# A parallel linear-attention and MLP kernel: later input tiles loaded behind the DMA transposes, the statistics of each tile finished before the previous tile is normalised, and the first MLP units of some tiles split

## The chip, the cores and the metric

The kernel runs on one core of one Trainium2 chip. The metric is the device time of one execution in microseconds (us); lower is better. The span of a profile, from its first to its last instruction, is about 1.75 us shorter than the time of the same execution. All runs compared here are in the fast state (granted TensorE clock 1.0) except one profile, which is named where it comes up.

## The reference, cut to what matters

```python
xn = layernorm(x)                      # x: 2048 x 640, bf16, eps 1e-5
out = x + attention(xn) + mlp(xn)      # both read the same normalised x
# attention: qkv = xn @ wqkv; phi(q), phi(k) with phi(t) = elu(t) + 1 + 1e-6;
#            32 heads of 20; o = phi(q) (phi(k)^T v) / (phi(q) sum phi(k) + 1e-6); o @ wo
# mlp:       gelu(xn @ w1 + b1) @ w2 + b2,  w1: 640 x 1536
```

## The kernel before

The 2048 rows are 16 tiles of 128. A tile goes through this line of stations before TensorE can use it: a load of x (SyncE's DMA queue), two `bn_stats` halves and a `bn_aggr` (VectorE), epsilon and the power -1/2 (GpSimd), the normalisation (VectorE), and a transposition into `xnT` (by TensorE for tiles 0 to 2, by DMA on SyncE's queue for tiles 3 to 15). While the tiles arrive, TensorE computes the first MLP product in units: one block of 128 of the 1536 features for one, two or four tiles. Each engine works through its own list in order (in the profile of before, VectorE normalises tile 7 only at 24.39 us, behind its wait for tile 8, although the rstd of tile 7 was there at 19.18), so the order in which the program writes its calls is the schedule.

```python
def ln_half(t, h):                 # VectorE: statistics of one half of tile t
    bn_stats(stats[:, s, ...], x_in[:, t, half h])
    if t < 2 and h == 0:           # GpSimd: epsilon goes in ahead of the aggregate (tiles 0, 1)
        stats[:, s, 2:3] += D * EPS
def ln_aggr(t):
    bn_aggr(aggr[:, s, :], stats[:, s, :])             # VectorE
    if t < 2: var = aggr[:, s, 1:2]
    else:     var = aggr[:, s, 1:2] + EPS              # GpSimd, all other tiles
    rstd[:, t] = var ** -0.5                           # GpSimd

# ... MLP units of tiles 0-3, one tile each ...
for t, n in ((4, 2), (6, 2), (8, 4), (12, 4)):         # then pairs, then fours
    plan += h_list(t, n, 0, JT)                        # JT = 12 feature blocks

def ln_rest():                     # called after tile 3
    for t in range(4, NT):
        if t + 1 < NT:
            ln_half(t + 1, 0); ln_half(t + 1, 1)
        ln_norm(t)
        if t + 1 < NT:
            ln_aggr(t + 1)
        xnT_dma(t)                 # DMA transpose
        if t == 5:
            dma_x(8, 4); dma_x(12, 4)
# ... (cut) then K, G, Q, the output product ...
```

Note that with this order the statistics of tile 8 stand ahead of the normalisation of tile 7 in VectorE's list.

## Time and profile before

| | before |
|---|---|
| median of the first 3 runs | 207.9 us (207.6 to 208.03) |
| the profiled execution | 208.43 us, span 206.7 us |
| TensorE busy | 98% of the span |
| MLP phase (first MLP matmul to the first K matmul) | 6.74 to 60.79 us |

The busy line of the page (busy time, share of the span, instructions):

```profile
PE 202.7 (98%) x1614; PEld 138.0 (67%) x1614; DVE 109.6 (53%) x227; ACT 73.6 (36%) x148; POOL 34.5 (17%) x85
```

TensorE bounds the kernel, so only its holes can be won. Matmul rows hide short holes: the profile's own legend says that the ends of matmuls are modelled, and the row at 34.73 below runs to 60.79 us, 0.17 us into the next, which starts at 60.62. So in the two views below, the matmul row at 34.73 admits 0.48 us of idling before it where the weight loads show 0.74, and the hole of 0.26 us at 27.24 is in no matmul row at all. The timeline of the matmuls, then that of the weight loads (start us, duration us, engine, line, operation, tiles; in brackets the idle time before the row and what ended it):

```profile
11.48 22.76 PE L388 MATMUL ps<-xnT,W 128*128 128x128 bf16 x285
34.73 26.06 PE L388 MATMUL ps<-xnT,W 128*128 128x512 bf16 x120 [0.48 <-DMA xnT<-xn_tm]
60.62 1.66 PE L490 MATMUL ps<-Wqkv,xnT 128*128 128x320 bf16 x11
```

```profile
11.43 15.81 PEld L388 LDWEIGHTS ps<-xnT,W 128*128 128x128 bf16 x225
27.50 6.46 PEld L388 LDWEIGHTS ps<-xnT,W 128*128 128x128 bf16 x60 [0.26 <-issue]
34.70 25.59 PEld L388 LDWEIGHTS ps<-xnT,W 128*128 128x128 bf16 x120 [0.74 <-issue]
```

The first 225 loads are the units of tiles 0-3 and of the pair 4-5, the next 60 the pair 6-7, the last 120 tiles 8-15. So TensorE waits at the pair 6-7 and again at tiles 8-11. VectorE's timeline shows why tile 7 is late (here and below, ... stands for rows left out):

```profile
17.66 0.45 DVE L361 TENSOR_SCALAR xn_tm<-xPK,aggr,rstd 128x640 bf16<-128x640 bf16 x1 [0.32 <-POOL rstd L349]
18.02 0.20 DVE L341 BATCH_NORM_AGGREGATE aggr<-stats 128x2 f32<-128x12 f32 x1
23.59 0.89 DVE L333 BATCH_NORM_STATS2 stats<-xPK 128x6 f32<-128x320 bf16 x2 [5.37 <-DMA xPK<-in_A_x_dram]
24.39 0.43 DVE L361 TENSOR_SCALAR xn_tm<-xPK,aggr,rstd 128x640 bf16<-128x640 bf16 x1
...
26.01 0.45 DVE L361 TENSOR_SCALAR xn_tm<-xPK,aggr,rstd 128x640 bf16<-128x640 bf16 x1 [0.32 <-POOL rstd L349]
```

The rows of L361 are the normalisations of tiles 6, 7 and 8. Tile 7 (24.39) had its statistics at 18.2, but waits for x8, for which VectorE idles 5.37 us. The 0.32 us before the other normalisations is the wait for rstd; it is part of the spacing of 1.63 us from tile to tile.

To measure holes I use one number for each profile, the *stretch*: from the end of TensorE's transposition of tile 2 to the start of K. Two lines of the chain of waits give its start and another its end (start us, duration us, what):

```profile
11.37 0.29 PE ps L369 x5
...
60.79 21.73 PE ps L490 x160
```

Here it is 60.79 - 11.66 = 49.13 us.

### The profile page before, as it was taken

The page shows a single profiled execution, that of the slowest core. Times are in us where ns is not written, and L with a number is a line of the kernel's source. Part 1 is how long each engine was busy: PE and PEld are TensorE (multiplying, and loading weights), DVE is VectorE, ACT ScalarE, POOL GpSimd, SP SyncE. Part 2 cuts the span into 40 slices and gives each one's busy share as a digit, 9 for nine tenths or more (in the row PEclk, how much of TensorE's full clock was granted, in tenths as well). Part 3 has the DMA queues.
Part 4 walks back from the last instruction along what each step waited for, and adds up shares of the span by engine and source line. Part 5 has one row for each costly group of instructions (what it writes and reads, how often), then busy time and mean ns, then how long its engine had stood idle before and what let it go on. Part 6 is the DMA issues. An engine that isn't in the chain of part 4 may idle for free.

```text
span 206.7 us, 4035 instructions
## 1 busy us (share of the span) xinstructions
PE 202.7 (98%) x1614; PEld 138.0 (67%) x1614; DVE 109.6 (53%) x227; ACT 73.6 (36%) x148; POOL 34.5 (17%) x85
## 2 busy tenths in 40 slices
PE   8999999999999999999999999999999999999995
PEld 3899886444457777777746445677777777777774
DVE  3784477100006888999448888744863322523322
ACT  2799886666667544211143554300000000000000
POOL 3233144710000000999100200000000000000000
DMA  5968975599920000000000000978611110010012
GB/s 149 347 175 75 278 100 101 97 353 324 376 86 0 0 3 0 3 0 0 0 3 2 0 0 10 342 202 165 164 67 52 43 35 32 32 36 32 32 36 62
DMA packets 24827, 19.70 MB, mean 95 GB/s; under 512 B 9960, under 2 KB 24808, under 8 KB 24808
## 3 DMA queue, kind: packets, MB, share of 16 engines
q1 hardware_dynamic: 23056, 17.86, 30.1%
q10 hardware_dynamic: 1752, 1.58, 4.1%
q8 instruction: 13, 0.21, 0.4%
q14 instruction: 6, 0.05, 0.1%
HBM read 13.11 MB, written 2.62 MB: 76 GB/s over the span
## 4 chain that ended last, share of the span: by engine, by line
PE 85%; DMA 5%; DVE 3%; POOL 3%; issue 2%; SPq 0%; ACT 0%; DVEq 0%
PE ps L673 36%; PE ps L388 15%; PE ps L490 11%; PE ps L515 11%; PE ps L556 10%; DMA xPK<-in_A_x_dram 4%; POOL rstd L349 2%; DVE stats L333 1%; DMA xnT<-xn_tm 1%; DVE aggr L341 1%; PE ps L610 1%; DVE xn_tm L361 1%; PE ps L566 1%; POOL veps L347 1%; PE ps L620 1%
## 5 line engine op out<-in xcount | busy, mean ns | idle before, releaser
L673 PE MATMUL ps<-W,HG 128*128 128x320 bf16 (+2 forms) x396 | 54.8, 295 | 0.0
L388 PE MATMUL ps<-xnT,W 128*128 128x128 bf16 (+2 forms) x480 | 53.3, 272 | 0.6 <-DMA xnT<-xn_tm 0.5
L388 PEld LDWEIGHTS ps<-xnT,W 128*128 128x128 bf16 x480 | 36.7, 98 | 16.6 <-issue 1.2
L673 PEld LDWEIGHTS ps<-W,HG 128*128 128x128 bf16 x396 | 38.1, 98 | 14.5 <-ACT Msb L592 0.2
L392 ACT ACTIVATE HG<-ps,b1c 128x128 bf16<-128x128 f32 (+2 forms) x96 | 41.5, 475 | 13.1 <-PE ps L388 11.5
L684 DVE TENSOR_TENSOR W<-ps,xnT 128x640 bf16<-128x640 f32 x15 | 12.4, 825 | 35.6 <-PE ps L673 35.0
L478 ACT ACTIVATE ek<-ps 128x512 bf16<-128x512 f32 (+1 forms) x36 | 23.2, 645 | 20.4 <-PE ps L556 10.3
L479 DVE TENSOR_SCALAR ek<-ek 128x512 bf16<-128x512 bf16 (+1 forms) x36 | 10.9, 304 | 31.9 <-ACT ek L478 30.7
L673 PE MATMUL ps<-Msb,PQ 128*128 128x320 bf16 (+2 forms) x165 | 24.2, 295 | 0.0
L556 PE MATMUL ps<-xnT,Wqkv 128*128 128x512 bf16 x100 | 21.9, 379 | 0.0
L490 PE MATMUL ps<-Wqkv,xnT 128*128 128x320 bf16 x160 | 21.9, 299 | 0.0
L515 PE MATMUL ps<-xPK,xn_tm 128*128 128x320 bf16 x160 | 21.9, 299 | 0.0
L673 PEld LDWEIGHTS ps<-Msb,PQ 128*128 128x128 bf16 x165 | 15.9, 98 | 5.9
L490 PEld LDWEIGHTS ps<-Wqkv,xnT 128*128 128x128 bf16 x160 | 15.7, 98 | 6.2
L515 PEld LDWEIGHTS ps<-xPK,xn_tm 128*128 128x128 bf16 x160 | 15.7, 98 | 6.1
L509 POOL COPY Wqkv<-Wqkv 128x128 bf16<-128x128 bf16 x25 | 15.1, 603 | 22.9 <-PE ps L490 21.4
L333 DVE BATCH_NORM_STATS2 stats<-xPK 128x6 f32<-128x320 bf16 x32 | 13.7, 467 | 8.7 <-DMA xPK<-in_A_x_dram 8.6
L556 PEld LDWEIGHTS ps<-xnT,Wqkv 128*128 128x128 bf16 x100 | 9.7, 98 | 11.4
L481 DVE SCALAR_TENSOR_TENSOR PQ<-ps,ek 128x512 bf16<-128x512 f32 x20 | 13.8, 691 | 2.1
L481 DVE SCALAR_TENSOR_TENSOR xPK<-ps,ek 128x640 bf16<-128x640 f32 x16 | 13.2, 825 | 1.7
L527 DVE TENSOR_TENSOR Msb<-Msb,xPK 128x640 f32<-128x640 f32 x14 | 11.6, 825 | 0.5
L519 ACT ACTIVATE W<-ps 128x640 bf16<-128x640 f32 x5 | 3.5, 704 | 18.2 <-PE ps L515 18.2
(59 smaller groups left out, 83.5 us busy)
## 6 DMA issues: line engine op xcount, KB each, us to landing
xnT<-in_A_x_dram SPq DMA_DIRECT2D x4, 640.0 KB, 6.3
Wqkv<-in_A_wqkv_dram SPq DMA_DIRECT2D x3, 800.0 KB, 6.9
out_dram<-W SPq DMA_DIRECT2D x15, 160.0 KB, 1.8
W<-in_B_w_dram SPq DMA_DIRECT2D x4, 480.0 KB, 6.0
W<-in_B_w_dram SPq DMA_DIRECT2D x1, 1920.0 KB, 13.3
xn_tm<-rden ACTq DMA_DIRECT2D x12, 128.0 KB, 3.4
xPK<-in_A_x_dram SPq DMA_DIRECT2D x2, 640.0 KB, 5.8
Wo<-in_A_wo_dram SPq DMA_DIRECT2D x8, 160.0 KB, 8.8
```

The lines of the kernel that those rows point to most:

```text
L333: Pl.ins(v, lambda e: e.bn_stats(stats[:, s, 6 * h:6 * h + 6], x_in[:, t, h * HW:(h + 1) * HW]), reads=r_x[t], writes=[r_stats[s][h]])
L388: Pl.ins(pe, [(lambda e, k=k: e.matmul(bank(b, 0, w), W1[:, k, jb * P:(jb + 1) * P], xnT[:, k, tok], start=(k == 0), stop=(k == DT - 1))) ...
L392: Pl.ins(s_, lambda e: e.activation(HG[:, jb, tok], bank(b, 0, w), ACT.Gelu_apprx_tanh, bias=b1c[:, jb:jb + 1]), reads=[B_[b], r_b1c], wri ...
L478: Pl.ins(s_, lambda e: e.activation(e2, src, ACT.Exp), reads=br, writes=[r_ek[s]])
L481: Pl.ins(v, lambda e: e.scalar_tensor_tensor(out=d2, in0=src, scalar=0.0, in1=e2, op0=ALU.max, op1=ALU.add), reads=br + [r_ek[s]], writes= ...
L490: fns.append(lambda e, k=k, h=h, b=b, t=t: e.matmul(bank(b + h, 0, HW), xnT[:, k, t * P:(t + 1) * P], Wqkv[:, k, D + h * HW:D + (h + 1) * ...
L509: Pl.ins(g, lambda e, k=k, i=i: e.tensor_copy(plain(Wqkv[:, k, D:2 * D], i), parts(Wqkv[:, k, 0:D], i)), reads=[r_Wq], writes=[r_Wk, r_WqP])
L515: Pl.ins(pe, [(lambda e, t=t, h=h, b=b, f=f, i=i: e.matmul(bank(b + h, 0, HW), xn_tm[:, t, f * P:(f + 1) * P], PK[:, t, h * HW:(h + 1) * H ...
L527: Pl.ins(v, lambda e, t=t: e.tensor_tensor(out=zsum, in0=zsum, in1=PK[:, t, :], op=ALU.add), reads=[r_PK[t], r_zsum], writes=[r_zsum])
L556: Pl.ins(pe, [(lambda e, k=k, j=j, b=b: e.matmul(bank(b), Wqkv[:, k, D + j * P:D + (j + 1) * P], xnT[:, k, cc], start=(k == 0), stop=(k == ...
L673: Pl.ins(pe, [(lambda e, i=i, x=x, bb=bb: e.matmul(bank(bb, 0, x[1] - x[0]), seq[i][0], seq[i][1][:, x[0]:x[1]], start=(i == 0), stop=(i = ...
L684: Pl.ins(v, lambda e: e.tensor_tensor(out=halves(out_sb[:, s, :]), in0=pair(b), in1=halves(x_res[:, t, :]), op=ALU.add), reads=B_[b:b + 2] ...
```

## The change

Its intent is to let the transposes of tiles 3-7 go ahead of the x8-15 loads, to give each rstd a whole tile of time (the statistics of tile t+1 are finished before tile t is normalised: one tile ahead), and to start tiles 4-5 and 8-11 on fewer tiles, so that the first units need fewer of them. The epsilon goes in ahead of the aggregate for every tile. The diff, cut to its core:

```diff
-            if t < 2 and h == 0:
+            if h == 0:
                 Pl.ins(g, lambda e: e.tensor_single_scalar(stats[:, s, 2:3], ..., D * EPS, ALU.add), ...)
...
-        for t, n in ((4, 2), (6, 2), (8, 4), (12, 4)):
-            plan += h_list(t, n, 0, JT)
+        plan += h_list(4, 1, 0, 2) + h_list(5, 1, 0, 2) + h_list(4, 2, 2, JT) + h_list(6, 2, 0, JT)
+        plan += h_list(8, 2, 0, 3) + h_list(10, 2, 0, 3) + h_list(8, 4, 3, JT) + h_list(12, 4, 0, JT)
 
         def ln_rest():
-            for t in range(4, NT):
-                ... (as shown above)
+            def out(t):
+                ln_norm(t)
+                xnT_dma(t)
+            ln_stats(5)
+            out(4)
+            ln_stats(6)
+            out(5)
+            ln_stats(7)
+            out(6)
+            out(7)
+            dma_x(8, 2)
+            dma_x(10, 2)
+            dma_x(12, 4)
+            ln_stats(8)
+            for t in range(8, NT):
+                if t + 1 < NT:
+                    ln_stats(t + 1)
+                out(t)
```

More of the change, by code (lines that the diff above doesn't have):

```diff
@@ L175, in bass_parallel_sum__linear_attn_block__dense_activation_gelu__prompt_kernel @@
         aggr = sb("aggr", [P, 4, 2], FP32)
-        veps = sb("veps", [P, 4], FP32)
         rstd = sb("rstd", [P, NT], FP32)
@@ L221, in bass_parallel_sum__linear_attn_block__dense_activation_gelu__prompt_kernel @@
         r_aggr = [R_("aggr%d" % i) for i in range(4)]
-        r_veps = [R_("veps%d" % i) for i in range(4)]
         r_rstd = [R_("rstd%d" % i) for i in range(NT)]
@@ L342, in ln_aggr @@
                    reads=r_stats[s], writes=[r_aggr[s]])
-            if t < 2:
-                var, r_var = aggr[:, s, 1:2], r_aggr[s]
-            else:
-                var, r_var = veps[:, s:s + 1], r_veps[s]
-                Pl.ins(g, lambda e: e.tensor_single_scalar(var, aggr[:, s, 1:2], EPS, ALU.add),
-                       reads=[r_aggr[s]], writes=[r_var])
-            Pl.ins(g, lambda e: e.tensor_tensor(out=rstd[:, t:t + 1], in0=var, in1=mhalf[:], op=ALU.pow),
-                   reads=[r_var, r_small], writes=[r_rstd[t]])
+            Pl.ins(g, lambda e: e.tensor_tensor(out=rstd[:, t:t + 1], in0=aggr[:, s, 1:2], in1=mhalf[:], op=ALU.pow),
+                   reads=[r_aggr[s], r_small], writes=[r_rstd[t]])
         def ln_stats(t):
@@ L419, in bass_parallel_sum__linear_attn_block__dense_activation_gelu__prompt_kernel @@
         plan += h_list(0, 1, 9, JT) + h_list(1, 1, 9, JT) + h_list(3, 1, 0, JT)
-        for t, n in ((4, 2), (6, 2), (8, 4), (12, 4)):
-            plan += h_list(t, n, 0, JT)
+        plan += h_list(4, 1, 0, 2) + h_list(5, 1, 0, 2) + h_list(4, 2, 2, JT) + h_list(6, 2, 0, JT)
+        plan += h_list(8, 2, 0, 3) + h_list(10, 2, 0, 3) + h_list(8, 4, 3, JT) + h_list(12, 4, 0, JT)
         def ln_rest():
-            for t in range(4, NT):
-                if t + 1 < NT:
-                    ln_half(t + 1, 0)
-                    ln_half(t + 1, 1)
-                ln_norm(t)
-                if t + 1 < NT:
-                    ln_aggr(t + 1)
-                xnT_dma(t)
-                if t == 5:
-                    dma_x(8, 4)
-                    dma_x(12, 4)
+            def out(t):
[13 more added lines that the diff above has]
+            for t in range(8, NT):
+                if t + 1 < NT:
+                    ln_stats(t + 1)
+                out(t)
         for u in plan:
```

## The prediction

> **What bounds the kernel now.** TensorE. The busy table gives PE 202.7 of 206.7 us (98%), and the chain of waits puts 85% on it. From 6.74 us its matmuls are almost unbroken there. The change touches only the MLP phase (line 388, 6.74 to 60.79 us), so only holes in those 54.05 us can be won.
>
> **The holes.** Back to back the matmuls cost 56 ns at width 128 (60 in 3.35 us in the chain) and 217 ns at width 512 (120 in 26.06 us). [...] The 128-wide units end at about 20.7 us (165 x 56 ns after 11.48). The 120 matmuls of width 256 should then take 13.1 us, but the first of width 512 starts at 34.73, so about 0.85 us are lost. The weight loads in the timeline show where: a hole of 0.26 us at 27.24 to 27.50 (tiles 6-7), one of 0.74 us ending at 34.70 (tiles 8-11; the matmul row admits only 0.48 of it, because ends are modelled).
>
> The first hole is tile 7. Its normalisation stands in the vector engine's order behind the statistics of tile 8, which wait 5.4 us for x8 (landed 23.59); so tile 7 is normalised at 24.84 and its DMA transpose lands at 27.5.  The second hole is tile 11: normalised 31.53, landed 34.39, wanted at 33.9.
>
> **What the change does.**
> - Tiles 4-7 no longer wait for x8. Vector work per tile is 0.83 + 0.20 + 0.45 us; the period is 1.63 with 0.32 us waiting for rstd. Two ahead, that wait goes: I estimate 1.5 to 1.55. Tile 7 is normalised near 18.6 and lands by about 23 (wanted 27.3): hole one goes.
> - x8-9 is issued at about 20.2 instead of 17.74, but is 320 KB instead of 640 KB and nothing competes with it. I estimate a landing at 23.5 to 24.5, thus no earlier than today. Tile 11 is then normalised at 30.9 to 31.8 and lands at 33.7 to 34.8: about as now.
> - The split of the first three units makes that harmless: tiles 10-11 are wanted only after 30 more matmuls of width 256 (3.3 us after tiles 8-9), at about 36 instead of 33.9. Hole two goes through the split, not through earlier data.
> - The merged epsilon removes no POOL work (two operations per tile remain), it moves one ahead of the aggregate.
> - [...] ScalarE gets 5 more activations, for which it has slack.
>
> Net: 0.85 - 0.06 = 0.8 us, all on the critical path; everything after the MLP phase simply shifts. Predicted 207.1 us (0.4% faster), range 206.6 to 207.8. Faster by over 2%: 0.005; same: 0.985; slower: 0.01.
>
> **What would show it.** The chain of waits should have no DMA transpose before the MLP matmuls of tiles 8-11; MLP should end at about 60.0 (60.79 before); weight loads should show no hole at 27 and 34; tile 7's normalisation at 18 to 19; phases after it the same length to 0.1 us.
>
> **What would make it wrong.** x8-9 landing after 25.5 would bring a new hole before tiles 8-9 or 10-11 and eat most of the gain; a shift of the PSUM ring by five units could add a wait at a phase border. None can exceed about 2 us.

The sum came to 0.85 - 0.06 = 0.8 us, and 207.9 - 0.8 = 207.1 us; the runs show the same 0.06 us (48.27 - 48.21, below). The 13.1 us is to be read as an estimate: a straight line through the two measured rates (56 ns at width 128, 217 at 512) gives 110 ns at width 256, 13.2 us for 120. before_delay below shows 39.00 us for 120 matmuls of width 256 and 120 of width 512; less the 26.06 us of the latter that is 108 ns each.

## The result, and the profile after

| | before | after |
|---|---|---|
| median, 6 runs each, same rounds | 207.88 us (207.6 to 208.26) | 207.72 us (207.37 to 208.18) |
| profiled execution, span | 206.7 us | 205.9 us |
| stretch | 49.13 us | 48.28 us |

The ratio is 0.9993, 95% interval 0.9978 to 1.0008: the same. Ratios here are the mean time of one kernel's fast runs over that of the other's of the same rounds, so not quite the ratio of the medians quoted. The two profiles differ by 0.8 us, the timings by 0.16 us.

The views after that answer to those of before: weight loads, VectorE from tile 6 on, and the chain of waits.

```profile
11.57 48.00 PEld L380 LDWEIGHTS ps<-xnT,W 128*128 128x128 bf16 x430
```

```profile
17.23 0.40 DVE L353 TENSOR_SCALAR xn_tm<-xPK,aggr,rstd 128x640 bf16<-128x640 bf16 x1
18.16 0.45 DVE L353 TENSOR_SCALAR xn_tm<-xPK,aggr,rstd 128x640 bf16<-128x640 bf16 x1 [0.53 <-POOL rstd L341]
24.29 0.89 DVE L331 BATCH_NORM_STATS2 stats<-xPK 128x6 f32<-128x320 bf16 x2 [5.68 <-DMA xPK<-in_A_x_dram]
...
28.32 0.40 DVE L353 TENSOR_SCALAR xn_tm<-xPK,aggr,rstd 128x640 bf16<-128x640 bf16 x1
...
29.74 0.39 DVE L353 TENSOR_SCALAR xn_tm<-xPK,aggr,rstd 128x640 bf16<-128x640 bf16 x1
...
31.16 0.40 DVE L353 TENSOR_SCALAR xn_tm<-xPK,aggr,rstd 128x640 bf16<-128x640 bf16 x1
```

```profile
11.51 0.28 PE ps L361 x5
11.79 48.27 PE ps L380 x430
60.07 21.73 PE ps L489 x160
```

All 430 weight loads are one row: no hole is left. Tile 7 is normalised at 18.16 instead of 24.39. The last three normalisations are tiles 9, 10 and 11, spaced 1.42 us. From the start of K to the end it is 205.9 - 60.07 = 145.8 us, against 206.7 - 60.79 = 145.9 before. In these two executions everything went as planned, and still the gain between the medians is a fifth of theirs, and not clear of noise.

### The profile page after: what moved, and what is told of

The parts are those of the page before. It is cut to its first block, busy times and chain, and to the rows that moved or that the text cites. A ratio compares the mean times of both kernels' runs of the same rounds, so it can differ in the third digit from the quotient of the medians.

```text
span 205.9 us, 4084 instructions
## 1 busy us (share of the span) xinstructions
PE 202.7 (98%) x1639; PEld 140.2 (68%) x1639; DVE 109.6 (53%) x227; ACT 74.6 (36%) x153; POOL 35.1 (17%) x85
## 4 chain that ended last, share of the span: by engine, by line
PE 98%; issue 0%; DVE 0%; ACT 0%
PE ps L672 36%; PE ps L380 26%; PE ps L489 11%; PE ps L514 11%; PE ps L555 10%; PE ps L302 2%; PE ps L609 1%; PE ps L565 1%; PE ps L619 1%; PE ps L318 0%; DVE W L723 0%; PE ps L361 0%; PE ps L538 0%; ACT b1c L310 0%; ACT xnT L326 0%
## 5 line engine op out<-in xcount | busy, mean ns | idle before, releaser
L380 PEld LDWEIGHTS ps<-xnT,W 128*128 128x128 bf16 x505 | 38.4, 98 | 14.1 <-issue 0.3
L384 ACT ACTIVATE HG<-ps,b1c 128x128 bf16<-128x128 f32 (+2 forms) x101 | 42.4, 463 | 11.3 <-PE ps L380 9.3
L508 POOL COPY Wqkv<-Wqkv 128x128 bf16<-128x128 bf16 x25 | 15.1, 603 | 22.9 <-PE ps L489 21.4
L480 DVE SCALAR_TENSOR_TENSOR xPK<-ps,ek 128x640 bf16<-128x640 f32 x16 | 13.2, 824 | 1.7
L341 POOL TENSOR_TENSOR rstd<-aggr,mhalf 128x1 f32<-128x1 f32 x16 | 9.9, 620 | 9.0 <-DVE aggr L339 9.0
```

Source lines behind the costliest of these rows:

```text
L380: Pl.ins(pe, [(lambda e, k=k: e.matmul(bank(b, 0, w), W1[:, k, jb * P:(jb + 1) * P], xnT[:, k, tok], start=(k == 0), stop=(k == DT - 1))) ...
L384: Pl.ins(s_, lambda e: e.activation(HG[:, jb, tok], bank(b, 0, w), ACT.Gelu_apprx_tanh, bias=b1c[:, jb:jb + 1]), reads=[B_[b], r_b1c], wri ...
L480: Pl.ins(v, lambda e: e.scalar_tensor_tensor(out=d2, in0=src, scalar=0.0, in1=e2, op0=ALU.max, op1=ALU.add), reads=br + [r_ek[s]], writes= ...
L508: Pl.ins(g, lambda e, k=k, i=i: e.tensor_copy(plain(Wqkv[:, k, D:2 * D], i), parts(Wqkv[:, k, 0:D], i)), reads=[r_Wq], writes=[r_Wk, r_WqP])
```

## The experiments

Theory A: the holes of before are there in every execution, and the timing merely has noise. Theory B: the one profiled execution of before was a slow one (208.43 us, while its timed runs lay at 207.6 to 208.26), and in usual executions x8 lands early enough that there is little or no hole to remove. Each kernel was timed in five rounds; its profile is the first execution of the six timed ones (only the first profile of before, 208.43 us, is not among the six of its table).

### Both kernels again

No edit.

> The kernel before once more, unchanged: a null measurement and a second profile. Theory A (the 0.85 us of holes in the MLP phase are there in every execution, and the timed gain of 0.16 us is small only through noise): ratio 1.000 within 0.001, the profile again has weight-load holes near 27.3 us (0.2 to 0.3) and 34 us (0.7), MLP phase 54.0 us. Theory B (the first profile caught a slow execution, 208.43 us against a median of 207.9, and the holes are smaller in most executions): ratio the same, but the profile shows an MLP phase of 53.3 to 53.8 us and smaller holes.

> The changed kernel once more, unchanged, for a tighter ratio. Theory A: 0.996 to 0.9975 (0.5 to 0.8 us faster). Theory B: 0.9985 to 0.9995 (0.1 to 0.3 us faster). Both: no holes in the weight loads from 11.5 us on, MLP phase 53.2 us.

Measured: before2 1.0002 (0.9988 to 1.0015), after2 1.0000 (0.9986 to 1.0015). Weight loads and x8 in the second profile of before:

```profile
11.50 22.25 PEld L388 LDWEIGHTS ps<-xnT,W 128*128 128x128 bf16 x285
34.25 25.59 PEld L388 LDWEIGHTS ps<-xnT,W 128*128 128x128 bf16 x120 [0.50 <-issue]
```

```profile
23.35 0.89 DVE L333 BATCH_NORM_STATS2 stats<-xPK 128x6 f32<-128x320 bf16 x2 [5.05 <-DMA xPK<-in_A_x_dram]
```

The same kernel, with x8 only 0.24 us earlier: the first hole is gone and the second is smaller; the stretch is 48.62 us instead of 49.13. Theory A falls: the holes are not a constant of the kernel. Against the changed kernel, whose stretch was 48.28 us again, 0.3 us is left, and even that the timing of after2 does not show. Its own execution began late: TensorE finished tile 2 at 12.04 us, after waiting for part of the MLP weight, against 11.65 to 11.86 in the other fast profiles.

### The two halves of the change

split_alone takes only the two lines of `plan`; order_alone takes everything but them.

> Only the MLP units are split (tiles 4 and 5 apart for two units, tiles 8-9 and 10-11 apart for three); loads and normalisation as before. My theory: the hole at tiles 8-11 (0.6 to 0.7 us) goes through the split alone, the one at tiles 6-7 (0.2 us) stays: MLP phase about 53.4 us, profile with one hole near 27.4. Rival (the earlier data is what fills the second hole): the hole stays and MLP phase is about 54.0.

> Only the order of normalisation and loads is changed, MLP units as before. My theory: the hole at tiles 6-7 goes, the one at tiles 8-11 stays at 0.4 to 0.8 us because tile 11 is normalised no earlier (31.5 us in the changed kernel's trace): MLP phase about 53.8 us. Rival (the order alone does it): no hole, MLP phase about 53.2.

Measured: split_alone 0.9998 (0.9984 to 1.0013), stretch 48.27 us, no hole. order_alone 1.0019 (1.0004 to 1.0033), stretch 48.63 us. Its weight loads and x8:

```profile
11.65 22.25 PEld L380 LDWEIGHTS ps<-xnT,W 128*128 128x128 bf16 x285
34.40 25.60 PEld L380 LDWEIGHTS ps<-xnT,W 128*128 128x128 bf16 x120 [0.51 <-issue]
```

```profile
24.33 0.89 DVE L331 BATCH_NORM_STATS2 stats<-xPK 128x6 f32<-128x320 bf16 x2 [5.65 <-DMA xPK<-in_A_x_dram]
```

order_alone is as I expected: the first hole is gone and the second stays. It is the half that costs time: behind two more transposes its load is issued at 20.96 us (17.74 in before) and x8 lands at 24.33 us, and TensorE still asks for tiles 8-11 all at once at 34 us. Its hole of 0.42 us is about what its timing is longer (0.0019 of 207.7 us, 0.4 us). In split_alone I expected the first hole to stay, and it did not. That says nothing for the split: x8 landed at 22.90 us in that execution, and at that landing tile 7 is in time in the old order too. Its rows for the weight loads and x8:

```profile
11.46 48.00 PEld L388 LDWEIGHTS ps<-xnT,W 128*128 128x128 bf16 x430
```

```profile
22.90 0.89 DVE L333 BATCH_NORM_STATS2 stats<-xPK 128x6 f32<-128x320 bf16 x2 [4.65 <-DMA xPK<-in_A_x_dram]
```

### What the holes are worth in time

before_delay puts 0.87 us of idle matmuls in front of tiles 4-5 of the kernel before. If holes of that size are there, the work is free.

```diff
+        plan += ["FILL"]                       # in front of the units of tiles 4-5
...
+            if u == "FILL":
+                filler(4)                      # 4 matmuls 128x512
```

> The kernel before with four idle 128x512 matmuls (0.86 us of TensorE work) put in front of the units of tiles 4-5: measures by time what the holes amount to in usual executions. Theory A (holes of 0.85 us in most executions): the delay is swallowed, ratio 1.000 to 1.001. Theory B (0.35 us or less): the time rises by 0.5 to 0.7 us, ratio 1.0025 to 1.0035. Theory C (no hole in most executions): full price, ratio 1.004. In the profile the holes at 27 and 34 us should be gone in every case.

Measured: 1.0036, interval 1.0021 to 1.0052. Of 207.8 us that is 0.75 us (0.44 to 1.08): of the 0.87 us nearly all was paid, and at most 0.43 was swallowed. Holes of 0.85 us in usual executions are excluded. The profile has no hole, and gives the stretch that this kernel has without one:

```profile
11.48 0.28 PE ps L369 x5
11.76 9.21 PE ps L388 x165
20.98 0.87 PE ps L304 x4
21.84 39.00 PE ps L388 x240
60.84 21.73 PE ps L493 x160
```

60.84 - 11.76 - 0.87 = 48.21 us. Against it the holes of before are 0.92 and 0.41 us in its two profiles, and the 25 additional matmuls of the split cost 48.27 - 48.21 = 0.06 us.

### The epsilon alone

```diff
-            if t < 2 and h == 0:
+            if h == 0:
...
-            if t < 2: ...  else: veps = aggr + EPS
+            var, r_var = aggr[:, s, 1:2], r_aggr[s]
```

> Only the epsilon is moved ahead of the aggregate for all tiles; loads, vector order and MLP units as before. Expected: rstd comes 0.3 us earlier after the aggregate (one POOL operation in the chain instead of two), so the vector period falls from 1.63 us towards 1.5 and tile 11 is ready about 1 us earlier; hole two shrinks to under 0.2 us. It also tests whether this part is why the three kernels with the new order end their PE transposition of tile 2 later (11.79, 12.05, 11.86 us against 11.66, 11.72, 11.68): if so it is late here too; if the late start is chance of the start phase, it is anywhere from 11.5 to 12.2.

Measured: 0.9994 (0.9976 to 1.0012). In its profile the spacing of the normalisations fell to 1.32 us, below the 1.42 of the changed kernel, and there is no hole at tiles 8-11. There is one at tile 7, nearly as large as both of before together. Two of its normalisations, VectorE's row for x8, then the weight loads after it:

```profile
29.25 0.45 DVE L356 TENSOR_SCALAR xn_tm<-xPK,aggr,rstd 128x640 bf16<-128x640 bf16 x1
...
30.57 0.45 DVE L356 TENSOR_SCALAR xn_tm<-xPK,aggr,rstd 128x640 bf16<-128x640 bf16 x1
```

```profile
24.33 0.89 DVE L333 BATCH_NORM_STATS2 stats<-xPK 128x6 f32<-128x320 bf16 x2 [6.92 <-DMA xPK<-in_A_x_dram]
```

```profile
28.28 32.15 PEld L383 LDWEIGHTS ps<-xnT,W 128*128 128x128 bf16 x180 [0.96 <-issue]
```

x8 landed at 24.33 us there, although it was issued at 17.36, earlier than before (17.74). The time of this execution was 208.56 us; the other five of the same kernel took 207.41 to 207.84. Take away the 0.87 us by which its stretch exceeds 48.21 us, and it is one of them (207.69). So a late landing of x8 is, as far as the times tell, something that some executions have and others don't. And before_late below, where x8 is there at 24.25 us and the first hole is as large (0.99 us), has a second hole of 0.65 us: at the same landing, the earlier rstd closes that hole without the split. The late end of tile 2 that I asked about (11.84 here) does not belong to the order: with the epsilon alone it is late as well, and after_late below, which has the whole change, ends it at 11.68.

### One idle matmul less at the start

```diff
-        filler(10)
+        filler(9)          # on top of split_alone
```

> The kernel with only the MLP units split, and nine instead of ten wide warm-up matmuls at the start. In both profiles of the changed kernel the warm-up matmuls ended at 5.9 us, after the first normalised tile was ready (5.6 to 5.7); with one less they should end by 5.5 [...]. Expected: 0 to 0.3 us faster than split_alone, ratio 0.9975 to 0.9995. [...]

Why the rate of these matmuls changes, no run here shows. The profiles show that they first run at half the later rate, at a granted clock of 1.0 throughout: one of width 512 every 0.43 us from 1.23 to 4.64 us in before and in after, against 0.217 us in the MLP. The last of the sixteen (ten wide, six narrow) ended at 5.43 us in before, at 5.91 in after, and in split_f9, with one wide one less, at 5.05. That they warm anything up, as their name in the expectation says, was not shown.

Measured: 0.9995 (0.9981 to 1.001), stretch 48.28 us, span 205.9 us as split_alone. Nothing to be told apart from split_alone; the expected gain is not shown. The profile says where it went: the MLP began 0.13 us earlier than in split_alone (6.52 against 6.65 us), but TensorE finished tile 2 at the same time (11.67 against 11.68 us).

### The place of the loads

```diff
+            dma_x(8, 2)
+            dma_x(10, 2)
+            dma_x(12, 4)
             ln_stats(7)
             out(6)
             out(7)
-            dma_x(8, 2)
-            dma_x(10, 2)
-            dma_x(12, 4)
```

> The changed kernel, but with the x8-15 loads issued right after the transpose of tile 5 instead of after that of tile 7 (still three loads, vector order and MLP units of the change). My theory: the place of the loads is worth nothing. The transposes of tiles 6-7 land later (some 4 to 6 us after issue instead of 2.6) but still before 27.3 us, x8 lands about 0.7 us earlier; no hole, stretch from the end of the third PE transposition to the end of the MLP 48.27 us as in the changed kernel, ratio within 0.001 of the changed kernel's. Rival: the loads in front of the transposes are what made hole one, and it comes back (0.2 us or more near 27 us).

> The changed kernel with the x8-15 loads right after the transpose of tile 5, a second time: its first profile fell into a slow state (granted clock 0.757), and its ratio of 0.9988 was the lowest of all. Expected: no hole in the profile, x8 landing near 23 us instead of 24.3 to 24.7, ratio 0.9985 to 1.0000, that is not to be told from the changed kernel.

Measured: early_x 0.9988 (0.9973 to 1.0003), with one of six executions, the profiled one, slow (266.83 us at a granted clock of 0.757; the other five 207.24 to 207.81). early_x2, the same kernel again, 1.0006 (0.9985 to 1.0027); the low first ratio was not repeated. In its profile there is no hole, and x8 lands almost 3 us earlier than in the changed kernel, where I had expected about 1 us (the weight loads, then x8):

```profile
11.61 48.00 PEld L380 LDWEIGHTS ps<-xnT,W 128*128 128x128 bf16 x430
```

```profile
21.44 0.89 DVE L331 BATCH_NORM_STATS2 stats<-xPK 128x6 f32<-128x320 bf16 x2 [2.80 <-DMA xPK<-in_A_x_dram]
```

So the first part of the change, the loads behind the transposes, delays x8 and gains nothing that these runs show; what frees tile 7 is the vector order. In the profile of before, issuing a transpose took SyncE 1.20 us in the median, against 0.51 us for the eight loads of x (0.40 to 1.73), and with the DMA engines busy throughout the transposes moved 209 GB/s in the mean (16.3 to 16.8 us), the x loads 381 GB/s (21.5 to 22.5 us). early_x2 has the earliest x8 of all; whether it would bear a forced delay better than the changed kernel was not tried.

### A late x8 on purpose

The last experiment forces what chance did in some executions. 0.49 MB of a weight are loaded right ahead of x8-15 (and again later, at their own place), in before, in split_alone and in the changed kernel.

```diff
+            dma("sync", W2[:, 0:3, :], <first 3 blocks of w2>, [r_W2])
             dma_x(8, ...)
```

> The kernel before with 0.49 MB of a weight loaded early (and again later at its own place), right ahead of the x8-15 loads, so that x8 lands later by an estimated 1.4 us (0.49 MB at the 350 GB/s of the trace). Theory T (the holes depend only on when x8 lands; in most executions x8 lands at about 23 us, just early enough, and the change therefore wins nothing there): now the holes are there in every execution, about 1.2 to 1.5 us in sum, ratio to the kernel before 1.005 to 1.008. Rival (the late landing of x8 is not the cause of the holes): within 0.001.

> The same early load ahead of x8-15 in the kernel with only the MLP units split. Theory T: tile 7 is still normalised behind the statistics of tile 8 and lands late, so a hole of 0.5 to 1 us opens at 27 us; tiles 8-11 come in time thanks to the split. Ratio to the kernel before 1.002 to 1.005.

> The same early load ahead of x8-15 in the changed kernel. Theory T: tile 7 no longer waits for x8 and the split gives tiles 8-11 about 1.5 us of reserve, so the delay is swallowed: no hole, or one of at most 0.3 us before tiles 8-9 or 10-11; ratio to the kernel before 0.999 to 1.0015. Rival (the change gives no protection): as before_late, 1.005 to 1.008.

Measured, in this order: 1.0089 (1.0063 to 1.0116), 1.0072 (1.0051 to 1.0093), 0.9998 (0.9979 to 1.0017). The weight loads, first of before_late, then split_late, then after_late:

```profile
28.13 6.46 PEld L388 LDWEIGHTS ps<-xnT,W 128*128 128x128 bf16 x60 [0.99 <-issue]
35.23 25.59 PEld L388 LDWEIGHTS ps<-xnT,W 128*128 128x128 bf16 x120 [0.65 <-issue]
```

```profile
28.84 32.18 PEld L388 LDWEIGHTS ps<-xnT,W 128*128 128x128 bf16 x195 [1.50 <-issue]
```

```profile
11.46 23.91 PEld L380 LDWEIGHTS ps<-xnT,W 128*128 128x128 bf16 x310
35.78 24.00 PEld L380 LDWEIGHTS ps<-xnT,W 128*128 128x128 bf16 x120 [0.40 <-issue]
```

And when x8 was there, in the same three kernels:

```profile
24.25 0.89 DVE L333 BATCH_NORM_STATS2 stats<-xPK 128x6 f32<-128x320 bf16 x2 [6.03 <-DMA xPK<-in_A_x_dram]
```

```profile
24.88 0.89 DVE L333 BATCH_NORM_STATS2 stats<-xPK 128x6 f32<-128x320 bf16 x2 [6.49 <-DMA xPK<-in_A_x_dram]
```

```profile
25.87 0.89 DVE L331 BATCH_NORM_STATS2 stats<-xPK 128x6 f32<-128x320 bf16 x2 [7.37 <-DMA xPK<-in_A_x_dram]
```

This is the mechanism of the prediction, now large enough to time. Before pays for a late x8 in both holes, in time a little more than I expected (1.0089 against 1.005 to 1.008); the profiled execution, 208.94 us, is one of its faster ones (median 209.48 us). With the split alone, the second hole closes but tile 7 still waits, and the hole at 27 us takes it all; it is larger than I expected (1.50 instead of 0.5 to 1 us), as x8 came 2.0 us later than in split_alone and not 1.4; so is its ratio (1.0072 against 1.002 to 1.005). With the whole change there is no hole at 27 us; x8 comes 1 us later still than in split_late, and only 0.40 us opens ahead of tiles 10-11. In time the changed kernel with the disturbance is as fast as the undisturbed one of before, while before loses 1.8 us.

All fast profiles together, with the holes as stretch minus 48.21 us (48.27 where the units are split; before_delay has none by definition, as the 48.21 us were taken from it):

| kernel | x8 there (us) | stretch (us) | holes (us) | span (us) |
|---|---|---|---|---|
| before, first profile | 23.59 | 49.13 | 0.92 | 206.7 |
| before2 | 23.35 | 48.62 | 0.41 | 206.2 |
| before_delay | 23.23 | 49.08 | none | 206.8 |
| eps_alone | 24.33 | 49.08 | 0.87 | 206.8 |
| split_alone | 22.90 | 48.27 | none | 205.9 |
| split_f9 | 22.88 | 48.28 | none | 205.9 |
| before_late | 24.25 | 49.67 | 1.46 | 207.2 |
| split_late | 24.88 | 49.69 | 1.42 | 207.4 |
| order_alone | 24.33 | 48.63 | 0.42 | 206.4 |
| after | 24.29 | 48.28 | none | 205.9 |
| after2 | 24.72 | 48.28 | none | 206.2 |
| early_x2 | 21.44 | 48.28 | none | 206.0 |
| after_late | 25.87 | 48.59 | 0.32 | 206.1 |

In the first eight rows, which have the old order of vector work and loads, the two with x8 at 22.9 us have no hole and each later landing leaves one, unless TensorE has been given other work first. But those two are split; a kernel without the split and with so early a landing was not profiled, so that it would have no hole at tiles 8-11 either is not shown. No version beats both kernels beyond the noise: the best two ratios, 0.9988 and 0.9993, have intervals that hold 1, and the first, run again, gave 1.0006.

## Why the prediction was right or wrong

The time was inside the range (207.72 us in 206.6 to 207.8, forecast 207.1) and the class was right, but the size was not: 0.8 us were forecast, and the timings show 0.16 us between medians, ratios of 0.9993 and 1.0000. That the time is in the range says little, as the range reached to within 0.1 us of the time of before.

- **"What bounds the kernel now": right.** From tile 2 to the end nothing but the holes differs between the profiles: 145.9 us from K to the end before, 145.8 after.
- **Where the holes come from: right.** Tile 7 behind x8, and tiles 8-11 asked for all at once. split_late, order_alone and before_late show each hole by itself and both together; after_late shows that the change closes the first and nearly closes the second.
- **"I estimate 1.5 to 1.55" for the spacing: too long.** It is 1.42 us, and 1.32 with the epsilon alone in the old order, so the new order was not needed for it. Moving the epsilon ahead of the aggregate, which I dismissed because it "removes no POOL work", takes an operation out of the chain from aggregate to rstd. Tile 7 was normalised by 18.61 us, as predicted (18.6).
- **x8-9 landing at 23.5 to 24.5: right for the profile (24.29), a little short for the second (24.72).** "Thus no earlier than today" was right too; early_x2 shows that the same loads land at 21.44 us if they are not put behind two transposes.
- **Tile 11 normalised at 30.9 to 31.8, the split making its lateness harmless, cost 0.06 us: right** (31.56, no hole, 0.06); that hole two goes only through the split was not, as eps_alone closes it too.
- **"0.85 - 0.06 = 0.8 us, all on the critical path": the step that failed.** The term 0.85 us (0.92 by the stretch) was read from one execution and taken for the kernel. In a second profile it was 0.41 us. The timed price of before_delay leaves at most 0.43 us of it in usual executions, with 0.12 (0.87 - 0.75) as the middle. A sign of it was there before the prediction: the profiled execution took 208.43 us, 0.4 us more than the slowest of the three timed runs (208.03). That the first two profiles agree with the 0.8 us is luck: the one of before was slow.

What stays open: how often x8 lands late in executions that were not profiled, and why. The profiles show landings of 22.88 to 24.33 us for loads issued at 17.36 to 17.85 us in the old order, but an execution without a profile shows only its time. That most of them land early is inferred from before_delay and from the five faster executions of eps_alone. A long time alone does not prove a hole: one execution of early_x2 took 208.6 us as well, and its profiled one has none. As to why, the six profiles of the old order with nothing put ahead of the loads give a hint, not a cause: in five, x8 was there 3.3 to 3.6 us after SyncE had finished issuing the two loads, which took it 1.70 to 2.29 us, and the longer that took, the later x8 was there. eps_alone is the exception: SyncE issued its loads in 1.13 us, yet x8 was there only at 24.33 us, 5.8 us after that; what held it up is not shown. Likewise, 0.1 us of true gain can't be told from none with these intervals.

## What to carry to other kernels

Before you cost a hole, compare the time of the profiled execution with the other runs: a hole that waits for a DMA can belong to that execution and not to the kernel (here 0.92 us of holes in one profile, 0.41 in the next), and a second profile is cheap. To price holes without trusting one trace, put a known amount of idle work in front of them: what is swallowed was a hole, what is paid was not (of 0.87 us here 0.75 was paid). A reordering that gives slack to late data need not make the usual run faster; test it by making the data late on purpose, where this one was worth 1.8 us.
